# Layer one's fourth weight group moved to the seven-product form, with the sums it needs begun earlier and added by GpSimd

## The chip, the cores and the metric

The kernel runs on one core of a Trainium2 chip. The metric is the device time of one execution in microseconds (us). A kernel is run several times and the median is compared. The engines of the core are named as in the profile: PE is TensorE (matrix products), PEld its weight loads, DVE is VectorE, ACT is ScalarE, POOL is GpSimd, SP is the engine that issues most transfers.

## The reference

A windowed attention gives `x` with 1536 tokens and 512 features. Two feed-forward layers follow:

```python
def _moe_ref(x, w_in, w_out):            # layer one, 2048 hidden features
    h = x @ w_in
    g = h * (1.0 / (1.0 + np.exp(-1.702 * h)))
    return g @ w_out

def _moe2_ref(x, w_gate, w_val, w_out):  # layer two, 1536 hidden features
    gate = 1.0 / (1.0 + np.exp(-(x @ w_gate)))
    val = x @ w_val
    return gate * val @ w_out
```

## The kernel before

**Blocks, groups, steps.** The tokens are cut into three blocks of 512 (0, 1, 2), layer one's hidden features into eight groups of 256 (0 to 7). A pair (group, block) is a step. Each fp32 operand is held as a high and a low part (`xH`, `xL`; `wH`, `wL`; `gh`, `gl`), and a product of two of them is three matmuls.

**A plain step.** `first(1, g, blk)` computes the 256 hidden features of the block: two products of 12 matmuls each (128x512). After each of them ACT takes the sigmoid, DVE multiplies (`gate_by`, L479), ACT casts the product to `gh` (L487) and POOL subtracts to get `gl` (L488). `second(1, g, blk)` multiplies `gh`, `gl` with the group's part of `w_out`: four results of 6 matmuls, each of which DVE adds to `acc` (L551). In each result the second and the fifth of the six matmuls are the ones that read `gl` first, of either half of the group. `second` of a step is issued one step late, behind `first` of the next step, so PE has 24 matmuls to do while `gl` is made.

**A group in the seven-product form.** `pair(1, g)` computes blocks 0 and 1 of a group together. It cuts weights and tokens in halves and forms seven half-size products of 6 matmuls (42) where the plain form has four times 12 (48). Block 2 stays plain (`single`). For this it needs sums of weight halves (`s`, made in `load`, L143 to L161: four small DVE operations, an ACT cast and a DVE subtraction) and sums of token halves (`tsum`, made once in `input_sums`). `PAIRED = 4`: groups 0 to 3 are plain, 4 to 7 use the seven products.

**The input sums.** `input_sums` is a generator. Its parts in order: `whole` of f1, of f3 (high part plus low part of a half block, 128x1024), f1 = f3 - f1, `whole` of f2, f3 = f2 - f3, f2 = f2 - f1, then low parts `l3` and `l1` on POOL (L250, L252), then a second `whole` of f3, f3 = f3 - f2, and low parts `l4`, `l2` on POOL (L262, L264); ACT makes the high parts. The name `folding` holds the generator, and `run`, the loop over a step's pieces, takes one part of it after each piece. The first eight parts are taken from one step on, the rest from step (1, PAIRED - 1, 1) on, because `h4` and `l4` are written over block 1's tokens.

**Order.** The order of the instructions on an engine comes from a scheduler that works from the order of the program and moves what it believes ready to earlier places; `keep_in_program_order` keeps an instruction behind the one that its engine was given just before it in the program. The weights' splitting (`load`: L125, L128, L132, L137 on DVE, L126 and L135 on ACT) runs ahead of its use through 14 places in SBUF; a place comes free when its group is done (`drop`). SP issues one weight transfer for each piece split.

In the plain steps the order on PE is: first(1,2,0), second(1,1,2), first(1,2,1), second(1,2,0), first(1,2,2), second(1,2,1), first(1,3,0), second(1,2,2), and so on to second(1,3,1); then pair(1,4) with second(1,3,2) between its products.

Of the kernel before, what the change touches and what calls it, by code (L numbers as in the profile page):

```python
# [14 lines left out]
ALU = mybir.AluOpType  # L15
# [14 lines left out]
def attention_moe_moe2_kernel(ctx: ExitStack, tc: tile.TileContext, ins: dict, out: bass.AP):  # L30
    nc = tc.nc
# [31 lines left out]
    xH, xL = [None] * NTB, [None] * NTB  # L63
# [17 lines left out]
    def pool(slots, n, name):  # L81
        p = ctx.enter_context(tc.tile_pool(name=name, bufs=n, reuse_waits="tile"))
        for s in slots:
            s.add(p, n)
        return p
# [4 lines left out]
    def places(n, name):  # L90

        p = ctx.enter_context(tc.tile_pool(name=name, bufs=1, reuse_waits="tile"))
        w_free.extend((p, f"{name}{i}") for i in range(n))
# [6 lines left out]
    def drop(*key):  # L100
        w_free.extend(w_held.pop(key))
# [7 lines left out]
    def load(layer, g, i, early):  # L109
# [29 lines left out]
        yield  # L139
        if layer == 1 and (g < PAIRED or i == 1) or layer == 2 and i == 2:  # L140
            yield
# [49 lines left out]

    mats = {1: [w_in, w_out], 2: [w_gate, w_val, w_out2]}
    pieces, weights, raws = [], {}, []
    PAIRED = 4
    wanted = [(1, g, i) for g in range(n1) for i in range(2)] + [(2, 0, 0), (2, 0, 1)]
    for g in range(n2):
        wanted += [(2, g + 1, 0)] * (g + 1 < n2) + [(2, g, 2)] + [(2, g + 1, 1)] * (g + 1 < n2)
# [22 lines left out]
    def t_tile(name):  # L220
        return tp.tile([P, KC // 2, TB], F32R, tag=f"t{name}", name=f"t{name}")

    def input_sums():

        def tt(**x):
            tc.keep_in_program_order(nc.vector.tensor_tensor(**x))

        f1, f2, f3 = (tp.tile([P, KC // 2, TB], F32, tag=f"f{n}", name=f"f{n}") for n in "123")  # L230
        h1, l1, h3, l3 = (t_tile(x) for x in ("1H", "1L", "3H", "3L"))

        def whole(to, blk, half):
            tt(out=to, in0=xH[blk][:, half], in1=xL[blk][:, half], op=ALU.add)

        whole(f1, 0, LO)
        yield
        whole(f3, 1, LO)
        yield
        tt(out=f1, in0=f3, in1=f1, op=ALU.subtract)  # L240
        yield
        whole(f2, 1, HI)
        yield
        tt(out=f3, in0=f2, in1=f3, op=ALU.subtract)
        nc.scalar.copy(h3, f3)
        yield
        tt(out=f2, in0=f2, in1=f1, op=ALU.subtract)
        nc.scalar.copy(h1, f1)
        yield
        nc.gpsimd.tensor_tensor(out=l3, in0=f3, in1=h3, op=ALU.subtract)  # L250
        yield
        nc.gpsimd.tensor_tensor(out=l1, in0=f1, in1=h1, op=ALU.subtract)  # L252
        yield
        h2, l2 = t_tile("2H"), t_tile("2L")
        h4, l4 = xH[1][:, LO], xL[1][:, LO]
        whole(f3, 0, HI)
        yield
        tt(out=f3, in0=f3, in1=f2, op=ALU.subtract)
        nc.scalar.copy(h4, f3)
        nc.scalar.copy(h2, f2)  # L260
        yield
        nc.gpsimd.tensor_tensor(out=l4, in0=f3, in1=h4, op=ALU.subtract)  # L262
        yield
        nc.gpsimd.tensor_tensor(out=l2, in0=f2, in1=h2, op=ALU.subtract)  # L264
        tsum.update({"1": (h1, l1), "2": (h2, l2), "3": (h3, l3), "4": (h4, l4)})
        yield
# [306 lines left out]
    def pull(n):  # L573
        for _ in range(n):
            next(coming, None)

    def need(*keys):
        for key in keys:
            tries = 0
            while key not in weights:  # L580
                pull(1)
                tries += 1
                assert tries < 100, (key, w_free, w_held)

    with tc.manual_schedule(engines={mybir.EngineType.SP}), ExitStack() as es:
# [192 lines left out]
        for _ in range(4):  # L778
# [28 lines left out]
            out=win, in_=win, pattern=[[0, NSLOT], [1, P - W0]], compare_op=ALU.is_gt, fill=NEG,  # L807
# [3 lines left out]
            out=win, in_=win, pattern=[[0, NSLOT], [-1, P - W0]], compare_op=ALU.is_gt, fill=NEG,  # L811
# [64 lines left out]
    with tc.manual_schedule(engines={mybir.EngineType.SP}):  # L876
        places(6, "w_b")
        pool([gh_slots, gl_slots], GF + 1, "g_b")
        pool([sg_slots], 5, "sg_b")
        acc_b = ctx.enter_context(tc.tile_pool(name="acc_b", bufs=1, reuse_waits="tile"))  # L880
        tp = ctx.enter_context(tc.tile_pool(name="tp", bufs=1, reuse_waits="tile"))
        ps_a, ps_b = (
            ctx.enter_context(tc.tile_pool(name=f"ps_{x}", bufs=n, space=PSUM, reuse_waits="tile"))
            for x, n in (("a", 4), ("b", 2))
        )
        ps_f, ps_s = Slots("h", (ps_a, 4)), Slots("h", (ps_h, 2), (ps_b, 2))
        folding, sums_1 = iter(()), input_sums()

        def run(main, rest=iter(()), after=()):

            for n, _ in enumerate(main):
                pull(1)
                next(folding, None)
                for _ in range(after.count(n)):
                    next(rest, None)
            for _ in rest:
                pull(1)
                next(folding, None)

        def seconds(layer, g, *blks):  # L900
            for blk in blks:
                yield from second(layer, g, blk, g == ends[layer])

        steps = [(1, g, 2) for g in range(2)] + [(1, g, blk) for g in range(2, PAIRED) for blk in range(NTB)]
        prev = None
        for step in steps:
            need((*step[:2], 0))
            run(first(*step))
            if step[2] == 2:
                drop(*step[:2], 0)  # L910
            if prev:
                need((*prev[:2], 1))
                run(second(*prev, False))
                if prev[2] == 2:
                    drop(*prev[:2], 1)
            if step == (1, 2, 0):
                folding = itertools.islice(sums_1, 8)
            elif step == (1, PAIRED - 1, 1):
                for _ in folding:
                    pass  # L920
                folding = sums_1
            prev = step
        top = n1 - 1
        for g in range(PAIRED, n1):
            need((1, g, 0), (1, g, 0, "s"))
            for _ in folding:
                pass
            if g < top:
                run(pair(1, g), second(1, g - 1, 2, False), (0, 2, 4, 5))
                drop(1, g - 1, 1)  # L930
            else:
                run(pair(1, g), seconds(1, g - 1, 1, 0), range(7))
            drop(1, g, 0, "s")
            need((1, g, 1))
            if g != top - 1:
                n = min(g, top - 1)
                run(single(1, n), seconds(1, g, 1, 0), (0, 0, 1, 1, 2, 2, 3, 3))
                drop(1, n, 0)
        folding = token_sums()
        run(single(1, top), second(1, top - 1, 2, False), range(4))  # L940
        drop(1, top, 0)
        drop(1, top - 1, 1)
        prev = (1, top)
        ps_f, ps_s = Slots("h", (ps_a, 4), (ps_b, 2)), Slots("h", (ps_h, 2))

        def ahead(g):
            if (2, g, 1, "s") not in weights:
                pull(1)

        for g in range(n2):  # L950
            need((2, g, 0), (2, g, 1), (2, g, 0, "s"), (2, g, 1, "s"))
            for _ in folding:
                pass
            rest = second(*prev, 2, prev[0] == 1)
            if g == 0:
                rest = itertools.chain(rest, half_sums())
            for slot, _ in enumerate(pair(2, g)):
                ahead(g + 1)
                if slot % 2 or g == 0 and slot:
                    next(rest, None)  # L960
                if slot % 4 == 3:
                    ahead(g + 1)
            for _ in rest:
                pass
            drop(*prev, prev[0])
            drop(2, g, 0, "s")
            drop(2, g, 1, "s")
            need((2, g, 2))
            rest = seconds(2, g, 0, 1)
            for _ in halves(g):  # L970
                ahead(g + 1)
                next(rest, None)
                ahead(g + 1)
            for _ in rest:
                pass
            drop(2, g, 0)
            drop(2, g, 1)
            prev = (2, g)
        for _ in second(*prev, 2, True):
            pass  # L980
# [40 lines left out]
```

## Time and profile before

| | |
|---|---|
| median of 3 runs | 622.05 us (621.97 to 622.18) |
| profiled execution, its own time | 621.5 us |
| its span, first to last instruction | 619.7 us |
| PE busy | 602.7 us, 97% of the span |
| DVE busy | 464.1 us, 75% |
| ACT busy | 309.1 us, 50% |
| POOL busy | 211.7 us, 34% |
| granted TensorE clock, mean | 0.997 of full speed |

Busy times of the engines overlap each other, so only the engine that others wait for sets the time at a moment. The profiled execution's own time is 1.8 us more than its span and 0.55 us less than the median of the runs.

### The profile page before, as it was taken

Reading aid. Unit: us, or ns where it says so; the run is one execution under the profiler, and the core shown is the slowest. Engines: PE = TensorE matmul, PEld = TensorE weight load, DVE = VectorE, ACT = ScalarE, POOL = GpSimd, SP = SyncE. Lnnn points to the kernel's source line nnn. Section 1 sums busy time; section 2 is a strip of 40 time slices with the busy share of each in tenths; the row PEclk is TensorE's granted clock in tenths of the full one; section 3 lists DMA queues with packets and bytes.
Section 4 is the critical chain, followed back from the end, with each engine's and each line's share of the span. In section 5 each row is a group of like instructions: output and inputs, shape, how many; then the busy total and the mean of one; then the engine's idle time right before and its main releaser. Section 6 shows DMA issues by size and latency. Waiting matters only on the chain.

```text
span 619.7 us, 8817 instructions
## 1 busy us (share of the span) xinstructions
PE 602.7 (97%) x3354; PEld 500.7 (81%) x3354; DVE 464.1 (75%) x684; ACT 309.1 (50%) x614; POOL 211.7 (34%) x168
## 2 busy tenths in 40 slices
PE   7798999999999999999999989999999999999997
PEld 4576887788878888888888878888898888888896
DVE  6799665489998878787669998357779668858434
ACT  4687757555434454435336557444435334435230
POOL 6797685223453323223322132022121132212030
PEclk9998999999999999999999999999999999999999
DMA  9998643044122203031001222211212222100014
GB/s 310 342 323 281 231 136 70 0 137 136 68 69 68 69 20 116 18 119 60 9 9 59 69 68 69 68 69 58 79 69 69 68 69 70 68 1 1 0 48 156
DMA packets 25161, 58.10 MB, mean 94 GB/s; under 512 B 1568, under 2 KB 1824, under 8 KB 25120
## 3 DMA queue, kind: packets, MB, share of 16 engines
q1 hardware_dynamic: 24400, 56.24, 27.7%
q10 hardware_dynamic: 720, 1.31, 0.6%
q8 instruction: 26, 0.43, 0.3%
q14 instruction: 15, 0.12, 0.1%
HBM read 53.08 MB, written 3.15 MB: 91 GB/s over the span
## 4 chain that ended last, share of the span: by engine, by line
PE 77%; DVE 10%; DMA 4%; issue 3%; POOL 3%; ACT 2%; SPq 0%; ACTq 0%; POOLq 0%
PE ps_o L468 31%; PE ps_y L173 14%; PE ps_v L173 9%; PE ps_x L173 9%; PE ps_h L468 6%; DMA xH<-in_moe_w_out 3%; PE ps_h L173 3%; PE ps_s L689 2%; PE ps_x L741 2%; DVE acc L551 2%; PE ps_p L722 1%; POOL gl L488 1%; DMA k<-in_k 1%; DVE sg L479 1%; DVE yL L558 1%
## 5 line engine op out<-in xcount | busy, mean ns | idle before, releaser
L488 POOL TENSOR_TENSOR gl<-sg,gh 128x512 fp32r<-128x512 f32 x84 | 126.6, 1513 | 364.7 <-ACT gh L487 245.1
L551 DVE TENSOR_TENSOR acc<-ps_o,acc 128x512 f32<-128x512 f32 x143 | 96.0, 685 | 50.6 <-PE ps_o L468 50.4
L487 ACT CAST gh<-sg 128x512 fp32r<-128x512 f32 x84 | 51.8, 622 | 50.4 <-DVE sg L479 42.3
L468 PE MATMUL ps_o<-gl,w_1H 128*128 128x512 f32 x192 | 75.8, 396 | 0.5 <-POOL gl L488 0.5
L468 PE MATMUL ps_o<-gh,w_1H 128*128 128x512 f32 x192 | 74.8, 391 | 0.0
L468 PE MATMUL ps_o<-gh,w_1L 128*128 128x512 f32 x192 | 72.4, 397 | 1.7 <-ACT gh L487 1.7
L468 PE MATMUL ps_o<-w_2L,gh 128*128 128x512 f32 (+1 forms) x146 | 56.7, 389 | 1.7 <-DVE w_2L L137 1.7
L468 PE MATMUL ps_o<-w_2H,gh 128*128 128x512 f32 (+1 forms) x146 | 56.4, 387 | 0.0
L468 PE MATMUL ps_o<-w_2H,gl 128*128 128x512 f32 (+1 forms) x146 | 56.0, 389 | 0.1
L132 DVE SCALAR_TENSOR_TENSOR da<-da,db 128x1024 uint32<-128x1024 uint32 x34 | 46.0, 1352 | 7.6 <-ACT da L126 7.1
L126 ACT ACTIVATE da<-da 128x1024 f32<-128x1024 f32 x34 | 36.1, 1062 | 19.9 <-DVE da L125 17.9
L468 PEld LDWEIGHTS ps_o<-gh,w_1L 128*128 128x128 f32 x192 | 36.2, 189 | 9.3 <-ACT gh L487 1.9
L468 PEld LDWEIGHTS ps_o<-gl,w_1H 128*128 128x128 f32 x192 | 36.4, 189 | 8.5 <-POOL gl L488 1.3
L468 PEld LDWEIGHTS ps_o<-gh,w_1H 128*128 128x128 f32 x192 | 36.2, 188 | 7.3
L702 ACT ACTIVATE e<-ps_s,nm 128x128 f32<-128x128 f32 x96 | 34.3, 378 | 8.3 <-DVE nm L694 7.2
L468 PE MATMUL ps_h<-xH,w_0L 128*128 128x512 f32 x96 | 37.7, 401 | 0.0
L468 PE MATMUL ps_h<-xL,w_0H 128*128 128x512 f32 x96 | 37.6, 392 | 0.0
L678 POOL TENSOR_SCALAR kx<-k 128x384 f32<-128x384 f32 x24 | 31.7, 1321 | 17.0 <-PE ps_s L689 8.6
L468 PE MATMUL ps_h<-xH,w_0H 128*128 128x512 f32 x96 | 37.5, 390 | 0.0
L468 PEld LDWEIGHTS ps_o<-w_2L,gh 128*128 128x128 f32 x146 | 27.5, 188 | 6.8 <-DVE w_2L L137 2.0
L479 DVE TENSOR_TENSOR sg<-ps_h,sg 128x512 f32<-128x512 f32 x32 | 21.8, 684 | 14.1 <-ACT sg L495 11.9
L468 PEld LDWEIGHTS ps_o<-w_2H,gh 128*128 128x128 f32 x146 | 27.4, 188 | 5.6
(242 smaller groups left out, 1501.6 us busy)
## 6 DMA issues: line engine op xcount, KB each, us to landing
raw<-in_moe_w_out SPq DMA_DIRECT2D x13, 1024.0 KB, 4.9
raw<-in_moe_w_in SPq DMA_DIRECT2D x8, 1024.0 KB, 7.1
raw<-in_moe_w_gate SPq DMA_DIRECT2D x6, 1024.0 KB, 5.0
raw<-in_moe_w_val SPq DMA_DIRECT2D x6, 1024.0 KB, 5.1
q<-in_q SPq DMA_DIRECT2D x20, 256.0 KB, 8.7
vwin<-in_v SPq DMA_DIRECT2D x6, 768.0 KB, 9.2
k<-in_k SPq DMA_DIRECT2D x8, 400.0 KB, 7.3
out<-acc SPq DMA_DIRECT2D x11, 256.0 KB, 2.0
```

The lines of the kernel that those rows point to most:

```text
L126: nc.scalar.activation(af, af, AF.Prelu, scale=REBIAS, alpha=-2.0 ** 32)
L132: nc.vector.scalar_tensor_tensor(out=a, in0=a, scalar=3, in1=b, op0=ALU.logical_shift_left, op1=ALU.bitwise_or)
L173: nc.tensor.matmul(ps, lhsT=a[x][:, kk, :], rhs=b[y][:, kk, :], start=start and i == 0, stop=i == n - 1, skip_group_check=True,)
L468: nc.tensor.matmul(ps, lhsT=a, rhs=b, start=i == 0, stop=i == n - 1)
L479: nc.vector.tensor_tensor(out=sg, in0=val, in1=sg, op=ALU.mult)
L487: nc.scalar.copy(gh, sg)
L488: nc.gpsimd.tensor_tensor(out=gl, in0=sg, in1=gh, op=ALU.subtract)
L551: nc.vector.tensor_tensor(out=a[:, m, :], in0=ps, in1=a[:, m, :], op=ALU.add)
L678: nc.gpsimd.tensor_scalar(out=to, in0=x, scalar1=scale, scalar2=None, op0=ALU.mult)
L689: nc.tensor.matmul(ps[:, j, :], lhsT=t[:, j, :], rhs=kt[:, j, :], start=False, stop=j == G - 1)
L702: nc.scalar.activation(e[:, j, :], s[:, j, :], AF.Exp, bias=nm[:, j:j + 1], accum_out=sm[:, j:j + 1])
L741: nc.tensor.matmul(ps[64 * e:64 * e + 64, j, :], lhsT=x[:, h * D:(h + 1) * D], rhs=y[:, j, 64 * e:64 * e + 64], start=n == 0, stop=n == le ...
```

## The change

`PAIRED` becomes 3, so that group 3 takes the seven-product form as well. The input sums' first eight parts are taken from step (1,1,2) on, where before it was (1,2,0); their rest from (1,2,1) on, where before it was (1,3,1), by the new value of `PAIRED`. The four additions of `whole` go from DVE to POOL, again kept behind what their engine was given before them.

```diff
-    PAIRED = 4
+    PAIRED = 3
...
         def whole(to, blk, half):
-            tt(out=to, in0=xH[blk][:, half], in1=xL[blk][:, half], op=ALU.add)
+            tc.keep_in_program_order(
+                nc.gpsimd.tensor_tensor(out=to, in0=xH[blk][:, half], in1=xL[blk][:, half], op=ALU.add)
+            )
...
-            if step == (1, 2, 0):
+            if step == (1, 1, 2):
                 folding = itertools.islice(sums_1, 8)
             elif step == (1, PAIRED - 1, 1):
```

## Rows read from the trace of the kernel before

**Rows 1.** The head of the page: span, and busy time of each engine.

```profile
span 619.7 us, 8817 instructions
...
PE 602.7 (97%) x3354; PEld 500.7 (81%) x3354; DVE 464.1 (75%) x684; ACT 309.1 (50%) x614; POOL 211.7 (34%) x168
```

**Rows 2.** Chain that ended last, in order of time: start, us, what.

```profile
178.90 3.70 POOL gl L488 x2
...
187.49 5.44 PE ps_h L468 x24
...
209.25 1.36 PE ps_x L173 x6
210.61 4.08 PE ps_o L468 x18
```

**Rows 3.** Timeline of PE: start, us, instruction, [idle before <-releaser].

```profile
142.76 0.39 PE L468 MATMUL ps_h<-xH,w_0L 128*128 128x512 f32 x1
...
180.84 0.39 PE L468 MATMUL ps_o<-gh,w_1L 128*128 128x512 f32 x1
...
182.65 0.50 PE L468 MATMUL ps_o<-gl,w_1H 128*128 128x512 f32 x1 [0.46 <-POOL gl L488]
...
187.32 0.39 PE L468 MATMUL ps_h<-xH,w_0L 128*128 128x512 f32 x1
```

**Rows 4.** Busy time in one stretch: PE, PEld, DVE, ACT, POOL, clock, DMA.

```profile
148.23:182.59 34.36, 33.96 (x149) 27.49 (x147) 32.87 (x36) 15.98 (x21) 18.62 (x9) 1.00 0.29 93
```

**Rows 5.** Timeline of POOL.

```profile
148.23 1.30 POOL L488 TENSOR_TENSOR gl<-sg,gh 128x512 fp32r<-128x512 f32 x1 [6.43 <-ACT gh L487]
...
164.67 3.42 POOL L252 TENSOR_TENSOR t1L<-f,t1H 128x1024 fp32r<-128x1024 f32 x1 [2.85 <-ACT t1H L248]
168.06 2.27 POOL L488 TENSOR_TENSOR gl<-sg,gh 128x512 fp32r<-128x512 f32 x1
...
176.53 2.41 POOL L264 TENSOR_TENSOR t2L<-f,t2H 128x1024 fp32r<-128x1024 f32 x1 [3.39 <-ACT t2H L260]
```

**Rows 6.** Timeline of DVE.

```profile
164.62 1.21 DVE L132 SCALAR_TENSOR_TENSOR da<-da,db 128x1024 uint32<-128x1024 uint32 x1
...
166.36 2.82 DVE L228 TENSOR_TENSOR f<-f,f 128x1024 f32<-128x1024 f32 x1
...
175.28 0.68 DVE L479 TENSOR_TENSOR sg<-ps_h,sg 128x512 f32<-128x512 f32 x1
...
177.08 1.27 DVE L551 TENSOR_TENSOR acc<-ps_o,acc 128x512 f32<-128x512 f32 x2
```

**Rows 7.** Groups by line and form, 148.2 to 182.6 us: count, busy, mean ns.

```profile
L551 DVE TENSOR_TENSOR acc<-ps_o,acc 128x512 f32<-128x512 f32 x11 | 7.3, 677 | 0.0
L228 DVE TENSOR_TENSOR f<-f,f 128x1024 f32<-128x1024 f32 x3 | 5.2, 1749 | 0.0
L132 DVE SCALAR_TENSOR_TENSOR da<-da,db 128x1024 uint32<-128x1024 uint32 x3 | 4.3, 1428 | 1.2 <-ACT da L126 1.2
...
L128 DVE TENSOR_SCALAR db<-raw 128x1024 uint32<-128x1024 uint32 x2 | 3.0, 1483 | 0.0
L137 DVE TENSOR_TENSOR w_1L<-da,w_1H 128x1024 fp32r<-128x1024 f32 x1 | 2.8, 2817 | 0.0
...
L125 DVE TENSOR_SCALAR da<-raw 128x1024 f32<-128x1024 f32 x2 | 1.4, 686 | 0.0
L160 DVE TENSOR_TENSOR s_0L<-ws,s_0H 128x1024 fp32r<-128x1024 f32 x1 | 1.2, 1226 | 0.4 <-ACT s_0H L158 0.4
L228 DVE TENSOR_TENSOR f<-xH,xL 128x1024 f32<-128x1024 f32 x1 | 1.2, 1216 | 0.0
...
L151 DVE TENSOR_TENSOR ws<-da,ws 128x256 f32<-128x256 f32 x1 | 0.4, 408 | 0.0
```

**Rows 8.** One line's instructions: ns least/median/most, first and last start.

```profile
L488 POOL TENSOR_TENSOR gl<-sg,gh x84: 1268/1302/2758, 56.3 to 609.7; 128x512 fp32r<-128x512 f32 x84
...
L228 DVE TENSOR_TENSOR f<-xH,xL x4: 1214/1217/2314, 140.6 to 192.4; 128x1024 f32<-128x1024 f32 x4
```

## Prediction

> **What bounds the kernel now.** The page's head comes first: PE is busy for 97% of a span of 619.7 us, DVE for 75%, POOL for 34% [rows 1]. A kernel like this gains only what PE has less to do, and loses whatever PE has to wait. The chain that ended last, read in order of time, then shows PE's pace, 24 matmuls in 5.44 us, so 0.227 us each [rows 2], and the one place in layer one's plain steps where the chain leaves PE: two `gl` subtractions on POOL, after which PE goes on at 182.65. PE's own timeline gives the size of that stall: second(1,2,2) begins at 180.84 and the next `first` at 187.32, which is 6.48 us for 24 matmuls that take 5.44, so 1.04 us are lost [rows 3].
>
> Why POOL was late is the question that the rest hangs on. From 148.23 (the first `gl` of group 2) to 182.59 (the last) DVE is busy for 32.87 of 34.36 us and POOL for 18.62 [rows 4]. Their timelines, laid beside each other, show that they keep each other out. POOL's 128x1024 subtraction takes 2.41 us at 176.53, while DVE does work on PSUM, and 3.42 at 164.67, when a DVE operation with two SBUF inputs had begun at 164.62 and ran 1.21 us [rows 5, 6]. DVE's subtraction at 166.36 takes 2.82 us where a free one of that size takes 1.22: it ends 1.1 us after POOL's operation has ended, at 168.09, and the `gl` that POOL began at 168.06 takes 2.27 where 1.30 is the median [rows 5, 6, 7, 8]. DVE's additions from PSUM (L551) keep 0.68 us whatever POOL does [rows 6, 7]. So in this stage there is a third resource beside the two engines: something that a POOL operation, or a DVE operation on SBUF operands, holds for its whole length. I call it the shared path.
>
> How full was it? From 148.23 to 182.59 POOL has six `gl` of 1.30 and three subtractions of 2.41, 15.0 us. DVE has ten two-input operations of 1024 columns (L228 four, L132 three, L137 two, L160 one) of 1.22, six of L151 at 0.41 and four of L125 and L128 at 0.69, 17.5 us; these are the unhindered durations [rows 5, 7, 8]. Together 32.5 of 34.36 us: the path was in use 95% of the time. That is what made the gate of (1,2,2) start at 175.28, though its matmuls were done near 167.2 (142.76 plus four phases of 5.44 and 12 matmuls), and what made its `gl` late [rows 3, 6].
>
> **The change part by part.** *Fewer matmuls.* Group 3's blocks 0 and 1 take 42 matmuls instead of 48: 6 times 0.227 is 1.36 us less on PE, which is the bound. Block 2 and `second` are the same.
>
> *Evacuations of the seven products.* Three more ACT copies and two DVE additions (0.68 each) in group 3. ACT is busy 15.98 of 34.36 us in the stretch above [rows 4], and this work falls into the steps after it, where PE waited for nothing: taken at nothing. Uncovered, the two additions would cost 1.4 us.
>
> *Weight sums of group 3.* Four L151, one L160 and an ACT cast: 4 times 0.41 plus 1.22, 2.9 us of DVE, near 140 us, where before the first two `whole` additions ran (2 times 1.22 unhindered). They change places with these [rows 7, 8], so DVE stands at 148 us as before: nothing, or the 0.5 us of difference on the new wait below if DVE has no gap there. Two of the 14 places are taken earlier, so (1,4,1) is split only once first(1,2,2) has freed places, near 170 us, and the transfers that SP issues behind it come as much later. It is not read before pair(1,4) has ended, 66 + 72 + 66 matmuls or 46 us after 175 us: nothing; were it due at once, its splitting (two operations of 0.69, two of 1.22) would cost 3.8 us.
>
> *The sums' start.* `whole` of f1 now stands behind the first `gl` of (1,2,0) on POOL, which ran at 148.23 [rows 5]. Before, DVE was given it later in the program and still ran it at 140.6 [rows 8], ahead of gates that stand before it. So the sums, which begin a step earlier in the program, begin 9 us later in time, and the stage that needs them comes 34 us sooner: P1, the first of the seven products, is due at 142.76 + 6 x 5.44 = 175.40 us instead of 209 [rows 2, 3].
>
> *The additions on POOL.* No row shows a 128x1024 addition on POOL. The nearest is the subtraction of the same size and kinds of operand, 2.41 us [rows 5]; the gates' `gl`, half the size, at 1.30 gives 2.60 as the upper bound, and DVE's 1.22 is the lower. I take 2.41. Each addition therefore takes 1.2 us more of the shared path than it did on DVE. The Trainium skill speaks against such a move in its page "Perfetto Trace Analysis", section "Optimizing Scalar/DVE Operations": GpSimd and VectorE share an SBUF read port, so shifting work between them may gain nothing. By the page alone the move would be worth about zero; by the rows it is a loss of 4 x 1.2 us of the path.
>
> *What is due when.* second(1,2,2) now comes right behind P1, as it did behind pair(1,4)'s [rows 2]: it begins at 176.76, and its fifth matmul, which reads the second `gl` of (1,2,2), at 177.67. Ahead of that `gl` on the path stand, from 148.23: on POOL six `gl` (7.8), the four `whole` (the last is kept behind the first `gl` of (1,2,2) and will be taken before the second, which is ready 2.7 us later), `l1` and `l3`, 6 x 2.41 = 14.5; on DVE the splitting and weight sums of (1,4,0) (L132, L137, L160, four L151) with one L125, and three of the sums' subtractions, 6 x 1.22 + 4 x 0.41 + 0.69 = 9.6. In all 31.9 us.
>
> - At the 95% that the path reached before: 33.6 us, ready at 181.8, PE waits 4.1 us.
> - Low end: the weight sums of (1,4,0) and the L125 slip behind (3.5 us less) and the path is never idle: 28.4 us, ready at 176.6, PE waits for nothing.
> - High end: `l2` is moved ahead, as it was at 176.53 [rows 5], and the L128 and L132 of the next weights too: 36.2 us at 95% is 38.1, ready at 186.3, PE waits 8.7 us.
>
> I take 4.1: it counts exactly what stands ahead in the program, at the use of the path that was measured. While PE waits, the sums' own rest (`l2`, f3, `l4`) goes on; it is due only at product 6 (the fourth) and at the last, some 6 and 11 us after 177.67, so it adds nothing unless the high end comes. Queued behind a late gate on DVE are the additions of second(1,2,1); PE has four PSUM banks before it needs them.
>
> The sum: -1.36 for the matmuls, -1.04 for the old stall, whose place is gone, +4.1 for the new one: +1.7 us. On the profiled execution 621.5 becomes 623.2; the median stands 0.55 above it, so 623.8 us.
>
> **The rivals.** A measurement of this kernel tells some 0.2%, or 1.24 us, from no change; so faster is below 620.8 and slower above 623.3.
>
> *The additions fit in.* POOL was idle for 15.7 of 34.36 us, and the scheduler may lay the four additions where DVE works from PSUM, whose operations keep their length [rows 4, 7]. It loses 4.9 us of DVE work too. Against it: the path was 95% full already. This decides when the second `gl` of (1,2,2) ends before 178.8, which wants 1.2 us of stall or less. Fully so the time is 622.05 - 1.36 - 1.04 = 619.65 us. Chance 0.30.
>
> *The stall only moves.* A new wait of 1.2 to 3.6 us eats the matmuls' 1.36 and the old stall's 1.04; about 622.0 us. For it: the full-use count without slips gives 2.5 us (31.9 from 148.23 is 180.1). Chance 0.22.
>
> *The pile-up.* `l2` and the next weights' splitting go ahead, and 8.7 us of stall give 628.4 us. For it: both stood ahead at 176.53 and just after in the trace of before [rows 5]. Against it: the next weights' places come free later now. Part of the slower side, 0.12 of its 0.48.
>
> **How the numbers follow.** The forecast (a stall over 3.6 us, most likely 4.1) has 0.48 with the pile-up, the stall that moves 0.22, the additions that fit in 0.30. The predicted time is the forecast's, 623.8. The range reaches from the full gain, 619.6, to the full pile-up, 628.4; inside the slower case it is 623.3 to 628.4. Faster 0.30, same 0.22, slower 0.48.
>
> **What the profile after would show.** The matmuls: six fewer, 3348 in all. The lock: `whole` on POOL at 2.4 us or more, first at about 149.5, and DVE's two-input operations near 150 to 178 often at 2 us or more. The stall: PE idle between P1 near 175.4 and the fifth matmul of second(1,2,2), released by POOL's `gl`, about 4 us. If `gl` is there by 177.7 and PE's row shows no idle time, the step on the shared path was wrong, and the likeliest reason would be the scheduler's order. If PE stalls elsewhere, on `l2` at product 6 or on an `acc` addition, the order of lateness was wrong. A shifted wait at the entry of layer two, from weights split in another order, would make the sum wrong without touching these steps.

## The result, and the profile after

The changed kernel takes 630.27 us (median of 4 runs, 629.7 to 630.61) beside 622.01 us of the kernel before on the same chip: a ratio of 1.0131 [1.0116, 1.0146] (in brackets, here and below, the 95% interval). That is slower, as forecast, but by 8.3 us where 1.7 were forecast, and above the top of the range (628.4). The profiled execution took 630.61 us, 9.1 us more than that of before, and its span is 9.1 us longer too. In the listing all lines after 232 stand two later than before: `gl` is L490, `acc` L553, PE's helper L470, and `whole` on POOL is L235.

The head of the page after (answers to [rows 1]):

```profile
span 628.8 us, 8816 instructions
...
PE 605.7 (96%) x3348; PEld 502.0 (80%) x3348; DVE 469.0 (75%) x687; ACT 309.6 (49%) x618; POOL 227.9 (36%) x172
```

PE has six matmuls less, yet is busy for 3 us more, and the span is 9.1 us longer. Where this lies, one view tells: the first matmul of layer one's plain steps, and the first of layer two, each the first start (the number behind the durations) of a row that groups one form of matmul. Of before:

```profile
L468 PE MATMUL ps_h<-xH,w_0H x96: 387/389/397, 41.1 to 203.4; 128*128 128x512 f32 x96
...
L173 PE MATMUL ps_x<-yH,w_0L x48: 277/336/400, 334.2 to 594.0; 128*128 128x512 f32 x24, 128*128 128x256 f32 x24
```

Of after:

```profile
L470 PE MATMUL ps_h<-xH,w_0H x72: 387/389/397, 41.3 to 169.8; 128*128 128x512 f32 x72
...
L173 PE MATMUL ps_x<-yH,w_0L x48: 277/336/400, 341.5 to 601.8; 128*128 128x512 f32 x24, 128*128 128x256 f32 x24
```

From the one to the other (called layer one below) it is 334.2 - 41.1 = 293.1 us before and 300.2 after, 7.1 more. From layer two's first matmul to the span's end it is 619.7 - 334.2 = 285.5 and 628.8 - 341.5 = 287.3, 1.8 more. As 1.36 us of matmuls and the old stall of 1.04 are gone, layer one lost 7.1 + 2.4 = 9.5 us somewhere, and the entry of layer two 1.8.

PE's timeline after shows both places (answers to [rows 3]; the starts of back-to-back matmuls are 0.227 apart at the full clock):

```profile
169.82 0.39 PE L470 MATMUL ps_h<-xH,w_0H 128*128 128x512 f32 x1
171.91 0.47 PE L470 MATMUL ps_o<-gh,w_1L 128*128 128x512 f32 x1 [1.69 <-DVE acc L553]
...
173.12 0.80 PE L470 MATMUL ps_o<-gh,w_1L 128*128 128x512 f32 x1 [0.28 <-ACT gh L489]
175.66 0.79 PE L470 MATMUL ps_o<-gl,w_1H 128*128 128x512 f32 x1 [1.75 <-POOL gl L490]
176.25 0.63 PE L470 MATMUL ps_o<-gh,w_1H 128*128 128x512 f32 x1
176.68 0.63 PE L470 MATMUL ps_o<-gh,w_1L 128*128 128x512 f32 x1
...
182.29 0.39 PE L173 MATMUL ps_x<-xH,w_0L 128*128 128x512 f32 x1
...
186.27 0.50 PE L470 MATMUL ps_o<-gh,w_1L 128*128 128x512 f32 x1 [1.55 <-DVE acc L553]
...
187.31 0.39 PE L470 MATMUL ps_o<-gl,w_1H 128*128 128x512 f32 x1
...
189.09 0.50 PE L470 MATMUL ps_o<-gh,w_1L 128*128 128x512 f32 x1 [0.70 <-DVE acc L553]
...
353.68 0.61 PE L470 MATMUL ps_o<-gl,w_1H 128*128 128x512 f32 x1 [2.92 <-POOL gl L490]
```

The last matmul of first(1,2,2) starts at 169.82, second(1,2,1) follows with three waits, P1 begins at 182.29 (175.40 was forecast), and second(1,2,2) behind it waits twice. Start to start, less the 0.227 of one matmul, the five gaps are 1.86, 0.44, 2.31, 1.71 and 0.86 us: 7.2. The rest of the 9.5 us is slow matmuls: from 176.25 to 179.66 eight of them start 0.427 apart, 8 x 0.20 = 1.6 us, and some right behind each gap. The windows show why (columns as in [rows 4], to which the first row answers):

```profile
148.23:182.59 34.36, 30.64 (x123) 24.18 (x123) 32.54 (x32) 13.70 (x19) 25.68 (x12) 0.90 0.21 72
...
170.00:172.00 2.00, 0.31 (x2) 0.12 (x2) 2.00 (x3) 0.55 (x1) 1.99 (x2) 1.00 0.00 0
172.00:174.00 2.00, 1.64 (x4) 0.65 (x4) 2.00 (x2) 0.62 (x1) 2.00 (x2) 0.76 0.72 225
174.00:176.00 2.00, 0.34 (x1) 0.34 (x2) 2.00 (x3) 1.49 (x2) 1.97 (x2) 0.50 0.73 299
176.00:178.00 2.00, 2.00 (x6) 1.52 (x6) 2.00 (x4) 0.06 (x1) 2.00 (x1) 0.50 0.00 0
```

PE is busy for 0.31 of the 2 us from 170; in the next 2 us the granted clock falls (0.76 on the mean), and from 174 it is 0.50, the lower of its two levels (1.2 GHz), also from 176 to 178, where PE works without a gap again.

POOL's timeline (answers to [rows 5]):

```profile
151.18 2.41 POOL L235 TENSOR_TENSOR f<-xH,xL 128x1024 f32<-128x1024 f32 x1
153.55 2.28 POOL L490 TENSOR_TENSOR gl<-sg,gh 128x512 fp32r<-128x512 f32 x1
155.78 5.11 POOL L235 TENSOR_TENSOR f<-xH,xL 128x1024 f32<-128x1024 f32 x2
...
168.34 2.27 POOL L490 TENSOR_TENSOR gl<-sg,gh 128x512 fp32r<-128x512 f32 x1
...
173.36 2.25 POOL L490 TENSOR_TENSOR gl<-sg,gh 128x512 fp32r<-128x512 f32 x1
175.63 3.29 POOL L266 TENSOR_TENSOR t2L<-f,t2H 128x1024 fp32r<-128x1024 f32 x1
...
184.49 2.25 POOL L490 TENSOR_TENSOR gl<-sg,gh 128x512 fp32r<-128x512 f32 x1
...
345.76 7.87 POOL L490 TENSOR_TENSOR gl<-sg,gh 128x512 fp32r<-128x512 f32 x1 [10.55 <-ACT gh L489]
```

DVE's timeline (answers to [rows 6]; the last seven rows are the entry of layer two, which the last section comes back to):

```profile
151.59 3.09 DVE L132 SCALAR_TENSOR_TENSOR da<-da,db 128x1024 uint32<-128x1024 uint32 x1
154.60 0.68 DVE L553 TENSOR_TENSOR acc<-ps_o,acc 128x512 f32<-128x512 f32 x1
155.20 3.44 DVE L151 TENSOR_TENSOR ws<-da 128x256 f32<-128x256 f32 x2
...
166.64 2.82 DVE L228 TENSOR_TENSOR f<-f,f 128x1024 f32<-128x1024 f32 x1
169.39 1.77 DVE L128 TENSOR_SCALAR db<-raw 128x1024 uint32<-128x1024 uint32 x1
171.08 0.68 DVE L553 TENSOR_TENSOR acc<-ps_o,acc 128x512 f32<-128x512 f32 x1
...
182.52 3.09 DVE L137 TENSOR_TENSOR w_1L<-da,w_1H 128x1024 fp32r<-128x1024 f32 x1
185.54 0.68 DVE L553 TENSOR_TENSOR acc<-ps_o,acc 128x512 f32<-128x512 f32 x1
...
345.55 1.21 DVE L280 TENSOR_TENSOR acc<-acc,acc 128x1024 f32<-128x1024 f32 x1
346.69 1.21 DVE L137 TENSOR_TENSOR w_0L<-da,w_0H 128x1024 fp32r<-128x1024 f32 x1
347.82 1.21 DVE L160 TENSOR_TENSOR s_0L<-ws,s_0H 128x1024 fp32r<-128x1024 f32 x1
348.96 1.21 DVE L287 TENSOR_TENSOR t2L<-acc,t2H 128x1024 fp32r<-128x1024 f32 x1
350.09 0.68 DVE L125 TENSOR_SCALAR da<-raw 128x1024 f32<-128x1024 f32 x1
350.69 1.21 DVE L287 TENSOR_TENSOR yL<-acc,yH 128x1024 fp32r<-128x1024 f32 x1
351.83 0.68 DVE L128 TENSOR_SCALAR db<-raw 128x1024 uint32<-128x1024 uint32 x1
```

The addition of `whole` takes 2.41 us when nothing is in its way. The `acc` additions for which PE waits are never slow themselves (0.68): at 171.08 and at 185.54 one stands directly behind an operation that POOL has held up, L128 with 1.77 for 0.69 us, `w_1L` with 3.09 for 1.22. How much of DVE's busy time is such waiting, the groups of 148.2 to 182.6 us tell (answers to [rows 7]: count, busy, mean ns):

```profile
L228 DVE TENSOR_TENSOR f<-f,f 128x1024 f32<-128x1024 f32 x3 | 6.2, 2077 | 0.0
...
L132 DVE SCALAR_TENSOR_TENSOR da<-da,db 128x1024 uint32<-128x1024 uint32 x2 | 4.8, 2388 | 0.0
L137 DVE TENSOR_TENSOR w_1L<-da,w_1H 128x1024 fp32r<-128x1024 f32 x2 | 4.3, 2158 | 0.4 <-ACT w_1H L135 0.4
L151 DVE TENSOR_TENSOR ws<-da 128x256 f32<-128x256 f32 x2 | 3.4, 1760 | 0.0
L128 DVE TENSOR_SCALAR db<-raw 128x1024 uint32<-128x1024 uint32 x2 | 3.4, 1720 | 0.0
...
L151 DVE TENSOR_TENSOR ws<-ws,da 128x256 f32<-128x256 f32 x1 | 2.0, 2010 | 0.0
```

Less their unhindered durations (1.22, 0.69 and 0.41 each) these six groups hold some 13 us in which DVE was counted busy and waited for POOL; 1.9 of them are in the `w_1L` of 182.52 to 185.61, behind the stretch, so 11 are in it. The same sum for before takes [rows 7] and two groups more of that view:

```profile
L151 DVE TENSOR_TENSOR ws<-da 128x256 f32<-128x256 f32 x4 | 3.1, 808 | 0.0
...
L137 DVE TENSOR_TENSOR w_0L<-da,w_0H 128x1024 fp32r<-128x1024 f32 x1 | 1.7, 1717 | 0.0
```

It gives 7.5 us. So DVE looks as busy as before (32.54 and 32.87 of 34.36 us) and did about 4 us less.

### The profile page after: what moved, and what is told of

Its sections match the earlier page's. It is cut to its first block, busy times and chain, and to the rows that moved or that the text cites. A ratio compares the mean times of both kernels' runs of the same rounds, so it can differ in the third digit from the quotient of the medians.

```text
span 628.8 us, 8816 instructions
## 1 busy us (share of the span) xinstructions
PE 605.7 (96%) x3348; PEld 502.0 (80%) x3348; DVE 469.0 (75%) x687; ACT 309.6 (49%) x618; POOL 227.9 (36%) x172
## 4 chain that ended last, share of the span: by engine, by line
PE 81%; DVE 9%; DMA 4%; ACT 3%; POOL 2%; issue 1%; SPq 0%; DVEq 0%; ACTq 0%; POOLq 0%
PE ps_o L470 33%; PE ps_y L173 15%; PE ps_v L173 10%; PE ps_x L173 9%; PE ps_h L173 4%; PE ps_h L470 4%; DMA xH<-in_moe_w_out 3%; PE ps_s L691 2%; PE ps_x L743 2%; DVE da L132 1%; PE ps_p L724 1%; DVE ws L151 1%; POOL gl L490 1%; DVE f L228 1%; DVE acc L553 1%
## 5 line engine op out<-in xcount | busy, mean ns | idle before, releaser
L490 POOL TENSOR_TENSOR gl<-sg,gh 128x512 fp32r<-128x512 f32 x84 | 134.1, 1604 | 356.3 <-ACT gh L489 261.9
L553 DVE TENSOR_TENSOR acc<-ps_o,acc 128x512 f32<-128x512 f32 x143 | 96.6, 684 | 48.9 <-PE ps_o L470 48.7
L470 PE MATMUL ps_o<-gl,w_1H 128*128 128x512 f32 x192 | 77.2, 402 | 4.7 <-POOL gl L490 4.7
L470 PE MATMUL ps_o<-gh,w_1L 128*128 128x512 f32 x192 | 73.1, 405 | 5.9 <-DVE acc L553 3.9
L470 PE MATMUL ps_o<-gh,w_1H 128*128 128x512 f32 x192 | 76.3, 397 | 0.0
L132 DVE SCALAR_TENSOR_TENSOR da<-da,db 128x1024 uint32<-128x1024 uint32 x34 | 49.2, 1448 | 11.4 <-ACT da L126 10.9
L470 PE MATMUL ps_o<-w_2L,gh 128*128 128x512 f32 (+1 forms) x146 | 56.6, 387 | 0.0
L470 PE MATMUL ps_o<-w_2H,gh 128*128 128x512 f32 (+1 forms) x146 | 56.4, 386 | 0.0
L470 PE MATMUL ps_o<-w_2H,gl 128*128 128x512 f32 (+1 forms) x146 | 55.9, 389 | 0.1
L470 PEld LDWEIGHTS ps_o<-gh,w_1L 128*128 128x128 f32 x192 | 36.7, 191 | 15.1 <-DVE acc L553 3.1
L470 PEld LDWEIGHTS ps_o<-gl,w_1H 128*128 128x128 f32 x192 | 37.1, 193 | 13.0 <-POOL gl L490 5.6
L470 PEld LDWEIGHTS ps_o<-gh,w_1H 128*128 128x128 f32 x192 | 36.9, 192 | 7.6
L680 POOL TENSOR_SCALAR kx<-k 128x384 f32<-128x384 f32 x24 | 33.1, 1379 | 17.2 <-DMA k<-in_k 8.6
L128 DVE TENSOR_SCALAR db<-raw 128x1024 uint32<-128x1024 uint32 x33 | 30.9, 937 | 2.0 <-DMA raw<-in_moe_w_out 1.8
L691 PE MATMUL ps_s<-kx,q 128*128 128x128 f32 x192 | 28.7, 298 | 3.6 <-DMA q<-in_q 1.8
L470 PEld LDWEIGHTS ps_o<-w_2H,gh 128*128 128x128 f32 x146 | 27.4, 188 | 5.7
L691 PEld LDWEIGHTS ps_s<-kx,q 128*128 128x128 f32 x192 | 25.9, 206 | 7.2 <-POOL kx L680 3.4
L470 PEld LDWEIGHTS ps_o<-w_2L,gh 128*128 128x128 f32 x146 | 27.5, 188 | 5.1
L470 PEld LDWEIGHTS ps_o<-w_2H,gl 128*128 128x128 f32 x146 | 27.3, 188 | 5.3 <-DVE acc L553 0.3
```

Source lines behind the costliest of these rows:

```text
L128: ts(out=b, in0=tail, scalar1=29, scalar2=None, op0=ALU.logical_shift_right)
L132: nc.vector.scalar_tensor_tensor(out=a, in0=a, scalar=3, in1=b, op0=ALU.logical_shift_left, op1=ALU.bitwise_or)
L470: nc.tensor.matmul(ps, lhsT=a, rhs=b, start=i == 0, stop=i == n - 1)
L490: nc.gpsimd.tensor_tensor(out=gl, in0=sg, in1=gh, op=ALU.subtract)
L553: nc.vector.tensor_tensor(out=a[:, m, :], in0=ps, in1=a[:, m, :], op=ALU.add)
L680: nc.gpsimd.tensor_scalar(out=to, in0=x, scalar1=scale, scalar2=None, op0=ALU.mult)
```

## The experiments

Two theories stood against each other at first. *The path*: the work added to what DVE and POOL share made the stage late, and less of it, or its return to DVE, brings the time back. *Earlier due*: the stage is due 34 us sooner and would be late with the additions on either engine. All ratios are against the kernel before, run in the same job.

**The additions back on DVE, all else as changed** (e1).

```diff
-            tc.keep_in_program_order(
-                nc.gpsimd.tensor_tensor(out=to, in0=xH[blk][:, half], in1=xL[blk][:, half], op=ALU.add)
-            )
+            tt(out=to, in0=xH[blk][:, half], in1=xL[blk][:, half], op=ALU.add)
```

> The changed kernel with the four additions back on DVE. Theory of the shared path (a GpSimd operation and a DVE operation on SBUF operands keep each other out, and each addition holds this path 1.2 us longer on GpSimd): the path has 4.8 us less to carry and DVE is no longer held for 2.4 us at a time, so of the 9.7 us that TensorE waits between 170 and 190 us more than half goes, 622 to 626 us. Rival, the earlier due time alone (the sums are due 34 us sooner, whoever adds): as the changed kernel, 629 to 631 us.

Measured: 632.41 us (629.63 to 633.6), 1.0176 [1.0159, 1.0193]. Taking the additions away from POOL gives nothing back. PE's waits are still there in other places, 2.00 us for `gl` at 173.06 and 2.58 for `acc` at 183.42. The path by itself, as I had costed it, falls; the rival's 629 to 631 us is the nearer, though the median lies 1.4 us above it.

**The additions on POOL alone** (e2: `PAIRED = 4` and the start at (1,2,0), as before).

> The kernel before with the additions on GpSimd alone: group 3 plain, the old start. Shared path: the old wait of 1.0 us near 182 us grows to 3 to 6 us, 624 to 627 us, though nothing is due earlier. Rival, the earlier due time: no change, 621.5 to 622.5 us.

Measured: 626.63 us (626.06 to 630.45), 1.009 [1.0057, 1.0122]. Where the stage is not due sooner, POOL's additions do cost 4.5 us, as the path would have it: PE waits 3.12 us for `acc` at 183.70 and 0.81 for `gl` at 188.67, in place of the old 0.46 [rows 3]. The rival, no change without an earlier due time, falls here.

**The earlier start alone** (e3: `PAIRED = 4`, additions on DVE, start at (1,1,2)).

> The kernel before with the earlier place of the sums in the program alone (additions on DVE, group 3 plain). Shared path and earlier due time both: nothing gained or lost beyond 1 us, 621 to 623 us, since DVE already ran the additions ahead of their place. A rival, that the earlier place in the program is itself what upsets the scheduler's order: 625 us or more.

Measured: 624.86 us (623.33 to 625.79), 1.0047 [1.0031, 1.0062]. Neither theory expected this; the third expectation, 625 us or more if the earlier place itself upsets the scheduler's order, is the nearest. The start by itself costs 2.7 us, with one wait of 2.23 us for `gl` at 175.09. So each of the two edits that were run alone disturbs the stage (`PAIRED` was not changed alone), and in e1 as in the changed kernel the stage is late, whichever engine adds.

**The additions free to move on POOL** (e4: `keep_in_program_order` taken from `whole`).

> The changed kernel without the order constraint on the GpSimd additions, so that the scheduler may run them before the first gl of (1,2,0), where GpSimd is idle. Shared path: if the first additions move to before 148 us, 7 us of the path's load leave the crowded stretch and the time falls to 622 to 627 us; if the scheduler leaves them, 629 to 631 us. Rival, that GpSimd is merely the slower adder and its own queue is the limit: 628 us or more in either case, since the queue's work stays the same.

Measured: 633.67 us (632.66 to 634.51), 1.0189 [1.0172, 1.0206]. Left free, the additions did move, three of the four to before 135 us, and yet the order is worse: a wait of 5.01 us comes at 155.91 already, for ACT's `gh`. The path's 622 to 627 us is missed, and where `whole` was kept is not the cause. The rival's 628 us or more is met, but e1, which takes the additions out of GpSimd's queue and is no faster, speaks against that queue as the limit.

**No weight work given out in group 2's steps** (e5 with the additions on POOL, e6 on DVE). The weights of group 4 are split on DVE in the stretch, long before pair(1,4) reads them; e5 and e6 keep the program from asking for that work there.

```diff
+        hold = [False]
...
             for n, _ in enumerate(main):
-                pull(1)
+                if not hold[0]:
+                    pull(1)
...
+        HELD = [(1, 2, blk) for blk in range(NTB)]
         for step in steps:
+            hold[0] = step in HELD
```

> The changed kernel with no weight splitting asked for during the three steps of group 2 (it is caught up behind them). Shared path: some 9 us of DVE's SBUF work leave the stretch from 148 to 178 us, the additions on GpSimd fit, and the waits there fall from 9.7 to under 3 us: 621 to 625 us, unless the weights then come late in group 3 or 4. Rival, the earlier due time alone: 629 to 631 us.

> As the run before it, and the additions on DVE. Shared path: the lightest load of all, waits of 0 to 2 us between 170 and 190 us, 619.7 to 622 us, which would beat the kernel before. Rival, the earlier due time alone: 629 to 631 us.

Measured: 630.26 us (629.29 to 633.28), 1.014 [1.0112, 1.0168], and 630.5 us (627.5 to 631.8), 1.0129 [1.01, 1.0158]. Both miss what the path would have, and nothing was learned of the weights: the scheduler brought the splits forward to where they had been, so e5 is the changed kernel over again. The edit was no lever; e12 below makes it one.

**The last `gl` ahead of layer two on DVE** (e7).

```diff
-        nc.gpsimd.tensor_tensor(out=gl, in0=sg, in1=gh, op=ALU.subtract)
+        eng = nc.vector if to[:3] == (1, 7, 2) else nc.gpsimd
+        eng.tensor_tensor(out=gl, in0=sg, in1=gh, op=ALU.subtract)
```

> The changed kernel with the two gl subtractions of step (1,7,2), the last of layer one, on DVE. In the changed kernel one of them stands 7.9 us on GpSimd, from 345.76 us on, while DVE runs seven SBUF operations without a gap, and TensorE waits for it some 2.9 us and runs at a lower granted clock for 3.5 us after. Theory that DVE's unbroken run shuts GpSimd out: 3 to 4.5 us less, 625.5 to 627.5 us. Rival, that this gl was late because its own input was late: 629.5 to 631 us.

Measured: 626.1 us (625.71 to 626.69), 1.0068 [1.0052, 1.0085], as expected. The wait at 353.68 is gone and the granted clock is 1.00 from 345 to 365, and the time from layer two's first matmul to the end falls from 287.3 to 282.8 us.

**The sums begun still earlier** (e8 on POOL, e9 on DVE): if the stage is only late, an earlier start should cure it.

```diff
+        folding = itertools.islice(sums_1, 8)
         for step in steps:
...
-            if step == (1, 1, 2):
-                folding = itertools.islice(sums_1, 8)
-            elif step == (1, PAIRED - 1, 1):
+            if step == (1, PAIRED - 1, 1):
```

> The changed kernel with the sums begun at the first plain step behind the attention, (1,0,2), two steps earlier in the program, additions still on GpSimd. Theory of too much DVE and GpSimd work due in one stretch (the sums, two groups' weight splits and the step's own additions all fall between 148 and 185 us): the additions go to 133 to 145 us, where GpSimd is idle, and of the 9.7 us that TensorE loses between 170 and 190 us at most 3 stay, 621 to 625 us. Rival, that the additions on GpSimd hold DVE up wherever they stand: 628 us or more.

> As the run before it, additions on DVE. Too much due in one stretch: DVE has 3.7 us more to do near 135 to 145 us, where it has gaps; 621 to 626 us. If the engine that adds mattered most, this would be the faster of the two by over 2 us.

Measured: 631.13 us (629.73 to 632.58), 1.0146 [1.0124, 1.0168], and 628.08 us (626.88 to 629.65), 1.0099 [1.0077, 1.012]. Both miss the 621 to 626 us, and e8 lies where its rival has it (628 us or more). e9 is the faster by 3.05 us, over the 2 us that were to mean that the engine that adds matters: at this start it does. e8's waits moved to 165.08 (4.02 us for `gh`) and 168.92 (2.42 for `gl`); e9 waits for nothing between 165 and 200 us, but 2.18 us for `acc` at 125.84 and 1.74 for ACT at 155.00. The load is moved about, not taken away.

**Without the split of group 4's weights** (e10; ACT copies stand in for it, and the additions are on POOL, as in the changed kernel).

> The changed kernel with the splitting of group 4's weights and its weight sums left out: ACT writes copies in their place, so DVE has some 10 us less to do on SBUF operands between 148 and 185 us (the values are not those of the reference). Too much due in one stretch: the losses of TensorE there fall from 9.7 to under 3 us, 621 to 624 us. Rival, that the order of GpSimd's queue alone makes gl and the sums late: 628 to 631 us.

Measured: 625.24 us (623.55 to 626.89), 1.0048 [1.0025, 1.007]: 5 us less than the changed kernel, so the splits were a good part of the load. The 621 to 624 us is missed all the same. Layer one still takes 295.1 us, with a wait of 2.14 us for `gl` at 174.39; the scheduler had put the split of the next weights, (1,5,0), into the free place at 153 to 163 us, which may be why. The wait at layer two's entry stays (2.93 us at 348.72).

**The kernel before, with that one `gl` on DVE** (e11; e7's edit).

> The kernel before with the two gl subtractions of step (1,7,2) on DVE. In the changed kernel this gave 4 us. If the entry of layer two in the kernel before loses time to the same cause (it waits 1.65 us for a weight split on DVE): 619 to 621 us. If it is only the order that the changed kernel gets there: no gain, 621.5 to 623 us, since DVE is full at that place.

Measured: 619.73 us (619.32 to 619.74), 0.9961 [0.9946, 0.9976]. This beats both kernels.

**All the work kept, but group 4's split held back until group 3** (e12 with the additions on POOL, e13 on DVE). Beside e5's edit, the first two operations of that split are kept behind what DVE was given before them, so that the scheduler can't bring them forward.

```diff
+        pin = tc.keep_in_program_order if (layer, g) == (1, 4) else lambda x: x
-        ts(out=af, in0=head.bitcast(F32), scalar1=F64_MAX, scalar2=-F64_MAX, op0=ALU.min, op1=ALU.max)
+        pin(ts(out=af, in0=head.bitcast(F32), scalar1=F64_MAX, scalar2=-F64_MAX, op0=ALU.min, op1=ALU.max))
...
-        ts(out=b, in0=tail, scalar1=29, scalar2=None, op0=ALU.logical_shift_right)
+        pin(ts(out=b, in0=tail, scalar1=29, scalar2=None, op0=ALU.logical_shift_right))
```

> The changed kernel with the splitting of group 4's weights kept behind step (1,2,2), so that none of it stands on DVE between 148 and 178 us; it is done in group 3 instead, and nothing is left out. Theory of too much DVE work due in one stretch, splits not yet needed among it: TensorE's losses between 170 and 190 us fall from 9.7 to under 3 us, and the time to 621 to 624 us, with the loss at layer two's entry still in it. Rival, that GpSimd's queue alone makes gl and the sums late: 628 to 631 us. Rival, that the split then comes too late for group 4: a new wait near 190 to 215 us of the same size.

> As the run before it, additions on DVE. Too much due in one stretch: within 1.5 us of the run before it either way, since an addition costs DVE 1.2 us itself or, on GpSimd, up to 2.4 us of waiting for GpSimd. If the engine that adds decides: over 3 us apart.

Measured: 622.11 us (620.99 to 623.46), 1.0002 [0.9993, 1.0012], and 622.35 us (621.41 to 623.39), 1.0008 [0.9998, 1.0018]. This is the run that tells: with one kind of work moved out of the stretch, and nothing left out, the 8.3 us are gone, and here it makes no difference which engine adds. e5, which has the same edit without the two pinned operations, is the control. In the profiles 6.8 us came back in layer one and 1.9 behind it, where e12 lacks the changed kernel's wait at the entry of layer two (table below). The same window in e12:

```profile
148.23:182.59 34.36, 34.36 (x153) 28.46 (x152) 23.46 (x26) 11.52 (x18) 27.14 (x14) 1.00 0.06 26
```

PE is busy throughout and DVE for 23.46 us where it was 32.54, with POOL as loaded as in the changed kernel. By the prediction's own count the shared path is as full in this window as it was before: on POOL six `gl` of 1.30, seven operations of 2.41 and 1.65 us of an eighth, on DVE five of 1.22, an estimate of 32.4 of 34.36 us or 94%. So a path this full need not make PE wait. The `gl` on which the prediction turned, on POOL, and the matmul that first reads it:

```profile
175.06 2.38 POOL L236 TENSOR_TENSOR f<-xH,xL 128x1024 f32<-128x1024 f32 x1
177.41 1.27 POOL L491 TENSOR_TENSOR gl<-sg,gh 128x512 fp32r<-128x512 f32 x1
```

```profile
179.69 0.39 PE L471 MATMUL ps_o<-gl,w_1H 128*128 128x512 f32 x1
```

It is there at 178.68. In this execution the plain steps begin 1.1 us later than before, so by the prediction's order it was due at 177.67 + 1.1 = 178.8. In fact the first four matmuls of the next result go ahead on PE, and it is first read at 179.69.

**The same with e7's edit** (e14 from e12, e15 from e13).

> The late split, additions on GpSimd, and the gl subtractions of step (1,7,2) on DVE. If the two losses (group 3's start and layer two's entry) are independent, the two gains add: 617 to 620 us, below both kernels. If curing one moves the wait to the other: 622 us or more.

> The late split, additions on DVE, and the gl subtractions of step (1,7,2) on DVE: 617 to 620 us if the two losses are independent, 622 us or more if not.

Measured: 620.07 us (619.75 to 620.97) and 620.5 us (619.29 to 621.23), both 0.9969 [0.9957, 0.9981]: no better than e11, which keeps group 3 in its plain form. They lie just above the 617 to 620 us that independent losses would give: the `gl`'s 2 us come off e12 and e13 as they come off the kernel before.

The two stretches of the accounting, worked out for these runs as for before and after, from the same two rows and the span:

| | plain steps to layer two | layer two to the end |
|---|---|---|
| before | 293.1 | 285.5 |
| after | 300.2 | 287.3 |
| e1, additions on DVE | 299.7 | 287.2 |
| e2, additions on POOL only | 297.7 | 285.5 |
| e3, start only | 295.6 | 285.5 |
| e7, after with the last `gl` on DVE | 299.9 | 282.8 |
| e11, before with the last `gl` on DVE | 293.1 | 282.6 |
| e12, late split | 293.4 | 285.4 |
| e14, late split and the last `gl` on DVE | 293.1 | 283.3 |

## Why the prediction was right in direction and wrong in size

*Fewer matmuls* and *the old stall*: right. 3348 matmuls, and no wait at the old place.

*The additions on POOL*: right. 2.41 us was taken and 2.41 measured, first at 151.18 where about 149.5 was expected. That DVE and POOL shut each other out is right as well: L132 at 3.09 us, L151 at 3.44 for two, L228 at 2.82.

*What is due when* is the step that failed. It took 4.1 us of stall, from the second `gl` of (1,2,2) alone, where layer one lost 9.5. The `gl` for which PE waits at 175.66 is the second of (1,2,1), a step earlier; the one that was priced ends at 186.74, and PE, held up until then, reads it at 187.31 without a wait. The count had two faults. It asked when the shared path would have done its work, but never went down DVE's own queue, which works in order (the `acc` addition at 171.08 is of a result whose matmuls PE had done by 164.8) and has no gap above 1.24 us from 150 to 189: what it waits for POOL is taken from all that stands behind, the additions from PSUM too. And it began at second(1,2,2), when second(1,2,1), one step earlier, was already late: PE's first wait ends at 171.91, 3.5 us before P1's forecast start, and is for an `acc` addition. The sentence that dismissed those, "PE has four PSUM banks before it needs them", is the one that was wrong; three of the five waits are for `acc`.

*Weight sums of group 3* had (1,4,1) split "near 170 us" at no cost, on the ground that it is not read for 46 us. It was split from 164.30 on (L125), L128 at 169.39, L132 at 175.00, `w_1L` at 182.52, and each stood in DVE's queue ahead of `acc` additions, L128 and `w_1L` directly ahead of two for which PE waited. That it isn't read soon does not make it free: what counts is what is queued behind it. e12 shows it: the same work, started after the stretch, and layer one is back at 293.4 us. It moves (1,4,0) with (1,4,1); which of the two weighs more was not run.

The rival of the *pile-up* described this (`l2` and the next weights' splitting go ahead: `t2L` runs at 175.63, ahead of the `gl` at 180.87) and with 8.7 us came closest (its 186.3 for the second `gl` of (1,2,2) beside 186.74), though it too had PE wait for that `gl`. It got 0.12, because I held it against it that the places for the next weights come free later. The *additions fit in*: e12 is that case for the `gl`, and even so it gains nothing. Of the 2.4 us, 2.14 go to two waits behind the stretch, 0.81 for `acc` at 203.32 and 1.33 for `gh` at 234.87. Around the first DVE is busy for 18.45 of the 20 us from 200 to 220, in before for 13.84; what made the second isn't shown.

Two terms were not in the sum. The low clock behind the waits, 1.6 us from 176.25 to 179.66. And the entry of layer two, which the prediction named as a thing that could make it wrong and didn't price: 1.8 us net. There the `gl` of (1,7,2) takes 7.87 us on POOL, from 345.76 to 353.63, and PE waits 2.92 us; the matmuls behind the wait are 0.4 us apart again. In before the same place has a wait of 1.65 us for `w_2L`. e7, which takes the shut-out away, is 287.3 - 282.8 = 4.5 us shorter there, and e11 shows that the kernel before loses 2.9 us at its own entry.

What stays open: why the earlier start alone (e3) costs 2.5 us of layer one, where the order of many operations on DVE differs from before; and why the shut-out at layer two appears in the changed kernel, e1, e4, e5, e6, e8, e9 and e10 (a wait of 2.92 or 2.93 us each), but not in e12 and e13, which have seven products in group 3 as well. The order of DVE's queue differs, more isn't shown.

The Trainium skill's sentence that the prediction weighed ("Perfetto Trace Analysis", section "Optimizing Scalar/DVE Operations": moving work between VectorE and GpSimd might not help) is borne out where the stage is full or empty, changed kernel against e1 and e12 against e13, and is too mild for e2, where the move costs 4.5 us, and for e8 beside e9, where it costs 3.05.

## What to carry to other kernels

When work is added to a full stretch, walk the in-order queue of each engine, operation by operation, and ask of each result that the bottleneck engine waits for what stands ahead of it; a sum over a shared resource finds when the whole is done, not when the one small addition behind it is. Work that is prefetched long before its use is not free in such a stretch, and moving it out can be worth more than changing who does the new work. Busy time hides waiting inside instructions: compare an instruction's mean with its fastest before calling an engine's load its work.

## What the runs showed of the hardware

DVE's operations on SBUF and POOL's hold each other up for a whole operation, and in most places of these traces the two engines take turns. At 151.59 L132 on DVE waits out one `whole` on POOL (to 153.59) and runs, and the `gl` behind that `whole` takes 2.28 us. The other way round, the `gl` begun at 168.34 waits out L228 on DVE (to 169.46) and gets in ahead of L128, though L128 stands directly behind L228: the `gl` takes 2.27 us and L128 1.77.

The entry of layer two is the clearest exception. In DVE's timeline above, seven operations on SBUF follow each other from 345.55 to 352.51, each at its unhindered length. POOL's `gl`, begun at 345.76, ends at 353.63, 1.1 us after the last of them: 7.87 us for an operation whose median was 1.30 [rows 8]. In the kernel before, at the same entry, a `gl` begun at 339.65 did get in between two such operations (it took 1.80 us, and the L285 behind it 2.32). What decides whether POOL gets its turn isn't shown.

The Trainium skill says in "SBUF — State Buffer", section "Who interferes with whom", that the pair of ports which DVE and GpSimd share is an exclusive lock, and of DVE's two-port modes that whoever issues first has the pair for the whole instruction while the other waits fully. The trace agrees on the whole instruction (L132 at 3.09 us, the `gl`s at 2.28 and 2.27); it does not on who goes first, as the `gl` of 345.76 began before six of the seven operations that kept it out. Of the operations with one SBUF input L128 takes part as well (1.77 us beside POOL, 0.69 alone); additions from PSUM keep 0.68.
